# An attention and mixture-of-experts kernel whose steps are issued in another listed order

## The chip, the core and the metric

The kernel runs on one core of a Trainium2 chip. The metric is device time in microseconds, the median of several runs of the whole program, from its inputs in HBM to its output in HBM. A core has five engines that run side by side and wait for each other through semaphores: TensorE (PE in the rows, its weight loads PEld), VectorE (DVE), ScalarE (ACT), GpSimd (POOL) and SyncE (SP), which here only issues transfers.

## What is computed

First a linear attention over 8 batches of 8 heads, 576 positions, head size 64, with a feature map of 128 columns that is used with both signs. Its output, heads side by side, is the input of a layer of four attention experts, of which each position uses two.

```python
def phi(x):
    proj = np.einsum('bhsd,df->bhsf', x, w_phi)
    proj = proj - np.max(np.abs(proj), axis=-1, keepdims=True)
    return np.concatenate([np.exp(proj), np.exp(-proj)], axis=-1)
q_p, k_p = (phi(q), phi(k))
kv = np.einsum('bhsf,bhsd->bhfd', k_p, v)
z = np.sum(k_p, axis=2)
num = np.einsum('bhsf,bhfd->bhsd', q_p, kv)
den = np.einsum('bhsf,bhf->bhs', q_p, z)[..., None] + 1e-06
x = num / den                          # then (batch, position, head * 64)
...
logits = x @ w_gate                    # the two largest of four, softmax over them
for e in range(4):
    q, k, v = x @ wq[e], x @ wk[e], x @ wv[e]
    scores = np.where(causal, -1e9, q @ k.transpose(0, 2, 1) / 8)
    ye = softmax(scores) @ v @ wo[e]
    out += weight_of_e * ye
```

## The kernel before

Two heads of one batch make a pair; there are 32 pairs (p), 16 pairs of pairs (m), and 8 batches (b) with two groups (g) of two experts. The work is cut into streams, written as Python generators, which run over these. Each `yield Step(engine, ...)` in one is a step: some instructions on one engine, with the PSUM bank that it needs. The streams that matter below:

- `load_k`, `load_q`, `load_v`, `load_tails`, `load_v_tails` and `weights` issue transfers on SyncE (the first two q loads on ScalarE). `k_in` and `q_in` have two buffers, `v_in` has one: `load_v` of pair p comes after the key-value product of pair p - 1 has read `v_in`.
- `stream_k`, `stream_q` and `stream_tails` project with `w_phi` (helper `half_mm`, L501). `center` and `evac_u` take the results out of PSUM, `phi_k` and `phi_q` make the exponentials. `evac_u` copies into `u` on ScalarE (L303) or VectorE (L315).
- `stream_kv` multiplies keys and values (L642), adds the column of key sums (L654), and turns the result; `stream_n` makes denominators (L740) and numerators (L751).
- `stream_b` projects to q and k of the experts and makes their scores (L294, L871), `stream_t` multiplies with the values (L1067), `project_out` makes the output, `store` writes it.
- `keep_warm` issues three small matmuls a step until the first pair's output is there.
- `key_sum` adds up key features for the sums in `zs`, by two transfers that accumulate (`add_to`, issued on GpSimd, L331): one of 512 KB for each pair from the fifth on, then one of 128 KB for the pair's tail.

The order in which these steps are issued is written out: `ORDER` has one character for each step, the place of a stream in the list of open streams, whose next step is issued then; a stream that ends leaves the list, a new one joins at its end. Each engine runs its own steps in that order. `SIDES` has a digit for each copy that either engine can make: 0 is ScalarE, 1 is VectorE. `Plan` keeps an account of estimated times as the steps are issued; from it, `Plan.loop` only takes which free PSUM bank is given next (the one that has been free for longest). What an estimate says of a transfer's issue therefore enters the program through the choice of a bank, and through the order that was found with it.

Of the kernel before, what the change touches and what calls it, by code (L numbers as in the profile page):

```python
# [16 lines left out]
B, H, S, D, F = 8, 8, 576, 64, 128  # L17
DM, E = 512, 4
# [45 lines left out]
def change_cost(a, b):  # L64
# [11 lines left out]
    r'FFBCE>?EHEH;AAG:6FF?DC8DD8D;2;5C@@ACBBB8:MIJBI::<IAGIC@FBH99F869FHDB8DCECB83CFBFBC088=DFEECBC8:68I8BFF70HG7IID'
    r'CG8D?5=B<GH6C4:99B2ECMEBEJA8J9886=GJD?>778CMI<HJKI>I<I@<BG39E9C18IHE<A@=8=?E?9G8857?7?EHAJJF083882HGF8ICDHC8DD'
    r'998:C6:GJHI>?I<:JG<1J:7IGH7J:KJGD:?<<BB:BE>@C>;GIIF>L;8>GJGIIJ;8<:=8:HJGHGGJ:IF::LGGK?I=N8=5:=>@K802GQJMM>F:I<'
    r':<0CEEBK=CFE::CFDCDDCJBICDCJCE=D9;;IJHJ<ICIKFHDF4883DD<8<G<<=BBBEI=CCDCDGEFEHGE8BB8D6A8>:I<C5:@@JJ@JEECIAD6BFI'
    r':JK:9FLH9MCLCIJGDHAF9BFAHD8IHBCIE880DH=28BHCB9;ADA@@CA@C@AEL@HB=ECD9;JJBBJD<BGFC;38772J7GF88GG?K=FD<CF895?==A3'  # L80
    r'=8EB888E67FE18D@KHJ@<0E@BCB28=E9988BBDIJID8DGB8848AF<B6<6EE57:7::G=HICLHE3DJDI:::;<BJGC>HD9GHG>B>GADEAF>EEE=8D'
    r'880@C?=B:98:DAF6DIEH8G8GBD9<:::GHHG7BB?NICL5H7B6N=EE;BGC@FI;G=E9?BDJEEBA:<::MGKKDBCG:GC=CD@BIGLMGKFBJH<G:=1348'
    r'8>?EI8IHCA=B;C<<<B>B28>:8:>>>JD>DL8DCBFKJE8::C=<FKEA5G8@:<=HFJHH9<>99AM=6HD?EK==K3@88028K7CJCLFNMKD>?<F?8G887?'
# [1108 lines left out]
```

## Time and profile before

| | us |
|---|---|
| median of three runs | 584.96 |
| the three runs | 583.71 to 586.16 |
| the profiled execution: device time | 583.6 |
| the profiled execution: span from first to last instruction | 581.6 |

The span is 2.0 us shorter than that execution's own time, which is 1.36 us below the median. The profile gives busy time by engine, by stretch and by line, who waited for whom, the chain of work that ended last, and each instruction in order of time. Times in it are counted from the start of the span. A matmul's end is modelled, so the distance between the starts of two steps tells more of TensorE than the length of one matmul.

### The profile page before, as it was taken

What the parts mean: (1) busy time and instruction counts of PE and PEld (TensorE: products, weight loads), DVE (VectorE), ACT (ScalarE), POOL (GpSimd) and SP (SyncE); (2) the same over time, 40 slices, a digit from 0 to 9 for tenths busy, and PEclk for the clock granted to TensorE, in tenths of its full rate; (3) what the DMA queues carried; (4) which work ended last, traced back from release to release, by engine and by line L of the source; (5) the groups of instructions that cost most, each with busy time, mean ns of one, the idle gap of its engine ahead of it and who ended that gap; (6) DMA issues with size and microseconds to landing.
All of it is one profiled execution on the core that took longest, in us unless ns stands there. A gap on an engine that the chain in (4) does not pass through costs nothing.

```text
span 581.6 us, 19193 instructions
## 1 busy us (share of the span) xinstructions
PE 568.9 (98%) x7655; PEld 440.1 (76%) x7655; DVE 531.6 (91%) x1150; ACT 454.4 (78%) x1109; POOL 287.3 (49%) x223
## 2 busy tenths in 40 slices
PE   7998999999999999999999999999999999999997
PEld 5664797678785779667876878867888677878886
DVE  7999899999999998999898989989999998898894
ACT  4999788878897969868878877989778678677562
POOL 4747472676337474365554457346635367331430
PEclk9999999999999999999999999999999999999999
DMA  6688546653446753593664664466556432311012
GB/s 163 153 193 200 118 102 156 151 117 93 98 114 149 175 122 53 141 230 72 147 151 101 156 134 107 98 159 134 131 130 146 114 87 46 90 58 42 1 57 109
DMA packets 55049, 69.74 MB, mean 120 GB/s; under 512 B 29232, under 2 KB 32688, under 8 KB 54960
## 3 DMA queue, kind: packets, MB, share of 16 engines
q1 hardware_dynamic: 48368, 49.58, 29.7%
q0 software_dynamic: 6272, 18.35, 19.5%
q8 instruction: 60, 0.98, 0.7%
q10 hardware_dynamic: 320, 0.59, 0.4%
q14 instruction: 29, 0.24, 0.1%
HBM read 35.59 MB, written 14.55 MB: 86 GB/s over the span
## 4 chain that ended last, share of the span: by engine, by line
PE 89%; DVE 5%; DMA 3%; ACT 2%; issue 1%; ACTq 0%; DVEq 0%; SPq 0%
PE ps_c L294 33%; PE ps_c L501 11%; PE ps_c L751 11%; PE ps_c L642 10%; PE ps_c L1067 7%; PE ps_c L871 7%; PE ps_c L740 5%; DMA v_in<-in_v_dram 2%; PE ps_c L654 2%; PE ps_c L607 2%; PE ps_c L1038 1%; DVE s L1000 1%; ACT s L303 1%; DMA q_in<-in_qt_dram 1%; DMA out_dram<-ot 0%
## 5 line engine op out<-in xcount | busy, mean ns | idle before, releaser
L713 POOL PARTITION_ALL_REDUCE mx<-u x64 | 145.7, 2299 | 66.2 <-DVE s L1000 17.1
L294 PE MATMUL ps_c<-x,qk 128*128 128x256 f32 (+1 forms) x768 | 108.0, 298 | 0.6 <-DVE yl L298 0.6
L294 PEld LDWEIGHTS ps_c<-x,qk 128*128 128x128 f32 x768 | 102.6, 189 | 4.4 <-issue 0.9
L979 POOL TENSOR_SCALAR_AFFINE_SELECT s<-s 128x256 f32<-128x256 f32 (+1 forms) x80 | 41.6, 557 | 79.5 <-ACT s L303 13.5
L305 ACT ACTIVATE ek<-ek 128x1024 f32<-128x1024 f32 x64 | 67.9, 1061 | 8.0 <-DVE ek L569 7.3
L996 POOL PARTITION_ALL_REDUCE max<-top x16 | 57.7, 3605 | 30.1 <-DVE top L992 14.4
L303 ACT COPY s<-ps_c 64x64 f32<-64x64 f32 (+4 forms) x141 | 52.9, 434 | 17.9 <-PE ps_c L871 17.6
L1000 DVE TENSOR_TENSOR s<-s,max 128x1152 f32<-128x1152 f32 (+4 forms) x80 | 65.6, 855 | 0.6 <-POOL max L996 0.6
L642 PE MATMUL ps_c<-ek,v_in 128*32 128x256 f32 x1024 | 61.7, 381 | 2.7 <-DMA v_in<-in_v_dram 2.7
L305 ACT ACTIVATE s<-s 128x384 f32<-128x384 f32 (+4 forms) x80 | 57.7, 742 | 7.4 <-DVE s L1000 7.1
L294 PE MATMUL ps_c<-yh,wo 128*128 128x256 f32 (+1 forms) x256 | 52.9, 300 | 0.0
L642 PEld LDWEIGHTS ps_c<-ek,v_in 128*32 128x32 f32 x1024 | 31.5, 110 | 25.8 <-DMA v_in<-in_v_dram 3.4
L331 POOL DMA_DIRECT2D zs<-ekt x28 | 23.6, 844 | 53.3 <-DVE zs L582 19.5
L294 PE MATMUL ps_c<-vg,x 128*128 128x260 f32 x384 | 49.0, 285 | 0.2 <-ACT s L303 0.2
L303 ACT COPY u<-ps_c 128x256 f32<-128x256 f32 (+1 forms) x107 | 40.6, 401 | 10.5 <-PE ps_c L501 9.9
L715 DVE TENSOR_TENSOR u<-u,mx 128x576 f32<-128x576 f32 x64 | 47.7, 760 | 0.4 <-POOL mx L713 0.4
L294 PEld LDWEIGHTS ps_c<-vg,x 128*128 128x128 f32 x384 | 47.1, 188 | 1.3 <-issue 0.5
L1067 PE MATMUL ps_c<-s,vs 128*32 128x320 f32 (+4 forms) x896 | 46.8, 357 | 0.0
L331 POOL DMA_DIRECT2D zs<-ek x28 | 25.4, 906 | 42.6 <-ACT ek L305 32.2
L566 DVE TENSOR_REDUCE pmax<-ps_c 128x4 f32<-128x512 f32 x64 | 42.5, 683 | 4.0 <-PE ps_c L501 3.5
L501 PE MATMUL ps_c<-q_in,wf 64*128 64x256 f32 (+1 forms) x256 | 42.9, 430 | 2.9 <-DMA q_in<-in_qt_dram 2.6
L305 ACT ACTIVATE mx<-u 128x576 f32<-128x576 f32 x64 | 43.3, 687 | 2.1 <-DVE u L715 1.8
(132 smaller groups left out, 1351.6 us busy)
## 6 DMA issues: line engine op xcount, KB each, us to landing
zs<-ek POOLq DMA_DIRECT2D x28, 512.0 KB, 5.5
out_dram<-ot SPq DMA_DIRECT2D x32, 288.0 KB, 2.8
q_in<-in_qt_dram SPq DMA_DIRECT2D x60, 144.0 KB, 3.6
k_in<-in_kt_dram SPq DMA_DIRECT2D x64, 128.0 KB, 3.5
v_in<-in_v_dram SPq DMA_DIRECT2D x32, 256.0 KB, 3.4
kvd<-kvt SPq DMA_DIRECT2D x104, 48.0 KB, 2.4
kv<-kvd SPq DMA_DIRECT2D x26, 192.0 KB, 2.6
zs<-ekt POOLq DMA_DIRECT2D x28, 128.0 KB, 3.3
```

What stands on the lines that cost most here:

```text
L294: nc.tensor.matmul(o, a, b, start=start, stop=stop, skip_group_check=True)
L303: nc.scalar.copy(o, i)
L305: nc.scalar.activation(o, i, func, **kw)
L331: nc.gpsimd.dma_start(o, i, accum_op=ALU.add)
L501: nc.tensor.matmul(o, a, b, start=True, stop=True, skip_group_check=True)
L642: nc.tensor.matmul(o[g, 0:2], v_in[:, 4 * h + t, k:64:2], ek[:, t, :, h, :].rearrange("p c (w f) -> p c w f", w=4), start=False, stop=t == ...
L713: nc.gpsimd.partition_all_reduce(M, U, 128, bass_isa.ReduceOp.absmax)
L715: dve(S, [uk], [mk], port=True).tensor_tensor(out=U, in0=U, in1=M, op=ALU.subtract)
L751: nc.tensor.matmul(ps[g:g + 32, 0:n], kvi[:, 2 * k + (h ^ p % 2), 32 * c:32 * c + 32], P_[h][c][:, s0:s1], start=c == 0, stop=c == 1, skip ...
L996: nc.gpsimd.partition_all_reduce(big.rearrange("p e s -> p (e s)"), top.rearrange("p e s -> p (e s)"), 128, bass_isa.ReduceOp.max)
L1000: dve(2 * (S - 128 * j), [('d', x, j)], [('max', z)], 1.11, True).tensor_tensor(out=block(s_, j, None, rows(j)), in0=block(s_, j, None, ro ...
L1067: nc.tensor.matmul(ps[r:r + 32, q0 - s0:s1 - s0], vs[:, j, 128 * g + 64 * e + k:128 * g + 64 * e + 64:2], ss[x][:, e, o + q0:o + s1], star ...
```

## The change

`ORDER` and `SIDES` hold other strings of the same length; two estimates of the planner's account are other numbers. Every stream has the steps that it had.

```diff
 ORDER = (
-    r'1110049B32894DDBBDCB726C8D99E1B8DF7GD4FEHDH000C=EDBF5CBBB9DC1934DEFE==E98H2=HIHHCED168E<=A541F<77DBIFJCEAE6AHH'
...
+    r'111111104923984CH2674GHG9DCEB5G8G8CE9BD4D327EIEHF=D9D9CBKCJB=FE9BHGE81==5H:HEBGG=9627GGKB1L:DC>CEDKE1E<IAFHFG<'
...
 SIDES = (
-    r'11110000111111000000001000011100000000110101100000001010001000000010010000110000000000000010000000000000000000'
...
+    r'10000000000101110010000000110000000000101000100010100010100000000010000000100000000000000000000000000100000000'
...
-    def add_to(o, i, w, r, issue=1220, part=1):
+    def add_to(o, i, w, r, issue=900, part=1):
         plan.transfer(o.free_size() * 128 * part / ADD_RATE, issue, w, list(r), 'POOL')
         nc.gpsimd.dma_start(o, i, accum_op=ALU.add)
...
         yield Step('POOL', pred=has('phi_t', m))
-        add_to(o[r], ekts[m % 2][r].rearrange("p c h f -> p (c h f)"), k, tk, 700, 0.5)
+        add_to(o[r], ekts[m % 2][r].rearrange("p c h f -> p (c h f)"), k, tk, 850, 0.5)
```

Unrolled, the lists can be compared. The 3118 steps are the same ones. `SIDES` has 520 digits, with 73 ones before and 60 after. Between the loads of `v_in` for pairs 4 and 5, SyncE issues before: k_in 6, q_in 7, q_in 8; and after: half of vg, half of wo, the other half of vg, q_in 7, the tails of keys 3. Of the `keep_warm` steps, three stand at the very start before and six after.

## Rows read from the trace of the kernel before

**Rows 1.** The page's first part: TensorE, weight loads, VectorE, ScalarE, GpSimd.

```profile
PE 568.9 (98%) x7655; PEld 440.1 (76%) x7655; DVE 531.6 (91%) x1150; ACT 454.4 (78%) x1109; POOL 287.3 (49%) x223
```

**Rows 2.** Sums by stretch: length, busy PE PEld DVE ACT POOL, clock, DMA share.

```profile
0.00:12.00 12.00, 8.24 (x86) 6.94 (x94) 8.24 (x38) 4.11 (x8) 3.85 (x7) 1.00 0.61 160
...
20.00:52.00 32.00, 31.71 (x562) 19.72 (x552) 31.00 (x64) 30.97 (x66) 18.55 (x12) 1.00 0.80 188
52.00:60.00 8.00, 5.61 (x79) 3.48 (x79) 6.41 (x12) 6.51 (x15) 5.33 (x4) 1.00 0.85 192
...
100.00:300.00 200.00, 199.48 (x2710) 152.40 (x2704) 188.37 (x403) 163.53 (x408) 108.45 (x85) 1.00 0.56 131
...
550.00:581.60 31.60, 26.61 (x321) 23.70 (x319) 23.71 (x55) 15.34 (x44) 7.39 (x6) 1.00 0.20 76
```

**Rows 3.** TensorE in order of time at the start.

```profile
1.05 1.14 PE L294 MATMUL ps_c<-warm 128*128 128x128 bf16 x9 [1.05 <-DVE col L338]
4.76 1.23 PE L501 MATMUL ps_c<-q_in,wf 64*128 64x256 f32 x4 [2.57 <-DMA q_in<-in_qt_dram]
...
11.06 0.68 PE L294 MATMUL ps_c<-warm 128*128 128x128 bf16 x9
```

**Rows 4.** What TensorE's matmuls waited for: total us, times, longest.

```profile
PE ps_c L642 <- DMA v_in<-in_v_dram: 2.7, 2, 2.4
```

**Rows 5.** The chain that ended last, 37 to 58 us: start, length, what.

```profile
37.92 1.73 PE ps_c L642 x32
...
47.88 1.91 PE ps_c L642 x32
...
49.80 6.45 DMA v_in<-in_v_dram
...
56.30 1.94 PE ps_c L642 x32
```

**Rows 6.** Groups by line: accumulating transfers, and the sums that read zs.

```profile
L331 POOL DMA_DIRECT2D zs<-ek x28 | 25.4, 906 | 42.6 <-ACT ek L305 32.2 <-ACT ot L303 4.4 <-DVE ge L936 3.8
L331 POOL DMA_DIRECT2D zs<-ekt x28 | 23.6, 844 | 53.3 <-DVE zs L582 19.5 <-DVE max L1012 7.4 <-DVE ql L824 7.3
...
L654 PE MATMUL ps_c<-zs,ones 128*32 128x128 f32 x224 | 11.4, 274 | 0.0
```

**Rows 7.** TensorE in order of time: numerator steps and the step behind them.

```profile
50.42 0.72 PE L751 MATMUL ps_c<-mx,kv 128*32 128x320 f32 x8
...
51.50 0.40 PE L654 MATMUL ps_c<-zs,ones 128*32 128x128 f32 x8
...
519.18 0.74 PE L751 MATMUL ps_c<-mx,kv 128*32 128x320 f32 x8
...
520.39 0.50 PE L294 MATMUL ps_c<-yh,wo 128*128 128x256 f32 x2
```

**Rows 8.** SyncE's issues in order of time, 40 to 55 us.

```profile
42.61 6.08 SPq L327 DMA_DIRECT2D q_in<-in_qt_dram  x4
49.80 0.34 SPq L327 DMA_DIRECT2D v_in<-in_v_dram  x1
...
53.53 1.18 SPq L327 DMA_DIRECT2D max<-in_wts_dram  x2
```

**Rows 9.** Loads of v_in: all 32, then the one at 341.6, GpSimd's transfer before.

```profile
DMA to landing us min/median/max: 2.6/3.4/6.4
...
L327 SPq DMA_DIRECT2D v_in<-in_v_dram x1: 346/346/346, 341.6 to 341.6; - x1
DMA to landing us min/median/max: 5.4/5.4/5.4
...
340.69 0.91 POOL L331 DMA_DIRECT2D zs<-ek  x1 [0.79 <-ACT ek L305]
```

**Rows 10.** Groups by line: copies into u, count, busy us, mean ns, idle before.

```profile
L303 ACT COPY u<-ps_c 128x256 f32<-128x256 f32 (+1 forms) x107 | 40.6, 401 | 10.5 <-PE ps_c L501 9.9
...
L315 DVE COPY u<-ps_c 128x320 f32<-128x320 f32 (+1 forms) x21 | 9.0, 448 | 2.8 <-PE ps_c L501 2.7
```

More of the change, by code (lines that the diff above doesn't have):

```diff
@@ new lines @@
+    r'E77AAE=D6FFH<<<=GBEBG9HE=AEGA9419352<914BEDA<F6E8GGGFJ83GHDDA7ADJ0;C;028B8A;;;JIBEFGA?:C5EEF3ED7C7?:?J6?E6EDCF'
+    r'DC@?::D;;A;:?DHAE8@F7FAAA7AD:EGKHE98GD@ED;AD;G::C?CG52173BG:HF@?:2G:9FFCFFG;EFDDDC67C0====FEEE@?:59AC=8JEH66@E'
+    r'?134D8<20H9GH9G>9CAF9<>EGAG@@B6:;:CBEDCEBC:?<8>D@BCCEFABA88;D?588I7FFJGF7;3HLFDDF;>;:;AMI>FEF?FF;E;@F@2;:E81EE'
+    r'AA00E@A@@8FG@>8DAGFE88E;8BDBBB8CC=;?5KDDBIIBH;KB6::CD=FIJA:9F9943808H88ACG6GCCFHG8@GH8:6J?8GI8D7JJFJ8EJHEF5:KF'
+    r'H<=>F<7E9E?GL>99NOF6@HD788I8IK6ANLAM78ACAKLJ@<>HHG3GH=D9<<>248DG98<=@<GG9>81?7==D78E=5I28DAFEEI=C<<IDD=8D8388C'
@@ new lines @@
+    r'D998>::6JKJHHF:IKIKFI=::7IGG=C<FK7I0::CAII=MENH<;;L<8LD<EKBKJIIFJE<8H::J:J?8J>=AEML=F:5:KLLIGO:LKJFI88::K:L@GM'
+    r'==>=KGEEECF8E8EF>JFEKFEGIE:;;>9;GDHEH=3FHBEECA6CDED002F<<<JBCH<HIHE<IEABABGA8F88A=DB:;5:J8L:ID:PMCD6JAMNAALEIA'
+    r'LDQQC0DKFC99GDBFG94GBEH3=CH8CEEDDKJHIJCDJH<BBE2FGCCB9B9AF@@DJ@GF=@EG;BH;7EHDHH=CC718888G?7B8BLG<8>>>82DFE839I5'
+    r'JD8786JK88JQJFG@HFFKF9489188K5KJKJGF8I=FDCF>L@<FF77OL6A<GHB6HC<EH=<:KC8083::::LMEMHJ>8C28:88G9L>BGKD>IEFFFAAEE'
+    r'89A@CC::<68GEEFHC9I?B1H8::;KJ=88838GD7CGJGHD5E7:BEGE=BGBAFLL=M6@6KBC;;9:I?:EE=><<FGH>>AFIGE@AJ::DD:I48H0IFI?H@'
@@ new lines @@
+    r'C?:HGFDCD??@B<FE<D><A?2@@@CB82=@=H8BBBFB?:<EA:I8BJ:K<?J5:9?CKJ3MAL90II8AC<F8LDGF98?7@HGGDCB088@@GE>>>F@8HHGDH7'
+    r'6F88?<BEKBKAGADH8EG99@A6HI9?IAH7?IF3;5KH@?IGJGB?<882@H<G>G48A8C>?D7=0>BJ=A=B<AI@<88;9B@F@9;G<J<JG8JJGGHA889FAB'
+    r'FE5>I:7:7?K0J23F<188HI88MMLH:H:GD:FH::E6FL?K89LEHCG9GJGGDG>HI8J8DI=GHGCF8:FEFHH;:<::JL:7DDGJR5?HP7ICKEQ6RJMN:S'
+    r'MME0QG83488822?EL=>:RJDBJNJOJCM8:EMGEEG:EE;?G;==DKIG6FCJG8JC89CKKD58HKLKJKGG@=EFF<<<<<IGGBBGB<MAE:::GEF9SE6LL>'
+    r'D99ANLNL8@:087QALB@7J881QE<3JCPPABLMH888:6EBJM8E=K@KKN8E999MD35JLL78N8N88MJSPOPOLCG?H?2=K=PO=8?8HJJ>H>899HHGKK'
@@ L101 @@
+    r'772847767664434330022270000;<95441877221716766466000096558085567<:;=9:857002055;:770077776:6756775751106655575'
+    r'900=0@04A:7?=97:;:=1181<99=7=977587188772215712531331111114442488552:12223951989077226616111101001515541412131'
+    r'00>?054=21>==11;3420807541611220242200'
 )
 SIDES = (
-    r'11110000111111000000001000011100000000110101100000001010001000000010010000110000000000000010000000000000000000'
-    r'00000000000000010000000000000000000000000000000000000000001000000000000000101001001000000000100000000000000000'
@@ L109 @@
+    r'00000000000000000000000001000100000000010000000001100000000010010000100000000000000000100000000100000100011000'
+    r'00000000001000000000000100000000000010100000000000100001010000000000000010000000000000000000001010100000000000'
+    r'00000100000100000000000101001000001000000100001000000000001000000000000000111100'
 )
```

42 lines of the change are left out of this document (11 added, 31 removed).

## The prediction, made from the kernel before alone

> **What bounds the kernel now.** I read the busy shares first [rows 1]. TensorE has a matmul in flight for 568.9 us of a span of 581.6 us, VectorE is busy for 531.6 us. The reader should see that only 581.6 - 568.9 = 12.7 us are left in which TensorE has nothing at all. Next I read the same sums by stretch, to see where these 12.7 us lie [rows 2]: 3.76 us in the first 12 us (12.00 - 8.24), 0.29 us from 20 to 52, 2.39 us from 52 to 60, 0.52 us from 100 to 300, and 4.99 us from 550 on; nearly all the rest, 0.8 us, is from 300 to 550. A kernel of which another order is tried can gain little more than these, and not all of them: the first stretch waits for the first q transfer (2.6 us, [rows 3]), and of the last 4.99 us some 4 us are the copy and the store behind the last matmul, which every order has. So TensorE bounds the kernel from 60 us on. From 20 to 52 it is different: VectorE is busy for 31.00 and ScalarE for 30.97 of 32.00 us there [rows 2], 97% each, with TensorE at 31.71. That stretch has three full engines.
>
> Then I read who TensorE waits for [rows 4]. One wait stands out: the products of L642 wait 2.7 us for v_in, twice, and 2.4 us of that in one piece. The chain of waits shows the piece [rows 5]: key-value product 4 ends at 49.8, the transfer of v_in for pair 5 takes from 49.80 to 56.25, and product 5 starts at 56.30. v_in has one buffer, so the load can't be issued before product 4 has read it; from there TensorE has other work until 53.9 and then stands still.
>
> The transfers that the change's words speak of, the accumulating ones, are not among these waits. Their issues take 906 and 844 ns on GpSimd [rows 6]; the sums that read their result (L654, out of zs) wait 0.0 us in 224 matmuls [rows 6]. The number put right in the planner is the price of something for which TensorE never waits in this trace. What the change can do, it does through the new order itself.
>
> **The change part by part.** Unrolled step by step, both lists hold the same 3118 steps. On TensorE 249 of 658 steps stand at the same place, the others have moved by 1.4 places in the mean; it is a near neighbour of the old order, not another one. Five things differ that can be priced.
>
> *Changes of TensorE's tiling.* The list before changes the shape of the array between neighbouring steps 181 times, the new one 176 times. Price of one change: the 320-column numerator step (16 matmuls, L751) takes 51.50 - 50.42 = 1.08 us where the next step has its own tiling, and 520.39 - 519.18 = 1.21 us where it has not [rows 7]: 0.13 us. Five fewer: -0.6 us. This lies on TensorE, so it counts in full.
>
> *The load of v_in for pair 5.* The stretch of TensorE work between product 4 and product 5 holds the same steps in both lists, 4.2 us. What differs is what SyncE issues ahead of the load. Before: k_in 6, q_in 7, q_in 8; the trace shows the four q_in issues drawn out from 42.61 to 48.69 (the last two wait for their buffer), so that q_in 8, 0.29 MB, goes out right in front of v_in at 49.80 [rows 8]. After: q_in 8 stands behind v_in, and ahead of it stand two halves of vg, one half of wo, q_in 7 and two small tails, 1.15 MB that wait for nothing late and can be gone before 49.8. On SyncE these are seven issues; two weight halves take 1.18 us to issue [rows 8], so the seven take some 4 of the 8.2 us from the end of product 3 (37.92 + 1.73) to the start of product 4 [rows 5], and the queue is free in time. The load then meets only the accumulating transfer of pair 5, which GpSimd issues at the same point of both lists. Bounds for its landing: 3.4 us is the median of the 32 loads; one load issued at 341.6, a microsecond after an accumulating transfer was issued at 340.69, took 5.4 us; the longest, this one, took 6.4 us [rows 9]. Against 4.2 us of cover the wait is 0, 1.2 or 2.2 us (2.4 in the trace). I take 5.4 us, the row with the same neighbour: -1.2 us, with 0 and -2.4 as ends.
>
> Here a page of the Trainium skill speaks against a larger gain: "DMA: Bandwidth & Descriptors", section "Queues, rings and completion order", says that each DMA engine takes turns between the queues that have work for it, a packet at a time. By that rule SyncE's order doesn't get v_in away from GpSimd's transfer, and the sum would be -1.2; by the median landing it would be -2.4.
>
> *Copies moved from VectorE to ScalarE.* SIDES has 73 ones before (a one is VectorE) and 60 after: 13 copies change sides. Eight of them are copies out of PSUM into u before product 5, in the stretch where both engines are full. One costs 401 ns on ScalarE and 448 ns on VectorE [rows 10]. With what is moved behind product 5, VectorE has 112 instructions up to there, not 123, and ScalarE 102, not 94. Of that the eight copies are -3.6 us on VectorE and +3.2 us on ScalarE. VectorE had most to do there, so its relief can let TensorE come earlier; ScalarE has only 1.03 us of idle time in 32 us [rows 2] to take them, but it has idle time while TensorE stands from 53.9 to 56.3. Ends: -2.4 us (two thirds of VectorE's relief passed on) and +3.2 us. I take -0.5 us. It is the least certain term.
>
> *Warm-up matmuls.* Before, nine stand at the start, nine at 11.06 and the last three later [rows 3]; after, eighteen stand at the start. Nine took 1.14 us there, so eighteen end at about 3.3 us, still ahead of 4.76, where the first q step starts [rows 3]. At 11.06 they took 0.68 us; but what follows them waits for ScalarE's exponential of the tail, so I cost their removal at nothing: the gap takes their place. Ends: -0.7 and 0.
>
> *Everything else*, the places of stores, masks, maxima and sums: each moves by a step or two. The small waits from 60 to 550 us add to some 1.3 us of idle time in the old order (0.52 + 0.8, [rows 2]); another order has others. 0 us, with -1 and +2 as ends.
>
> Sum: -0.6 - 1.2 - 0.5 = -2.3 us. The profiled execution took 583.6 us (span 581.6), and becomes 581.3. The median of the three runs, 584.96, lies 1.36 us above the profiled one; I forecast the median: 582.7.
>
> **The rivals.** (1) *Nothing to collect.* v_in for pair 5 still lands after 6.4 us, because the accumulating transfer and the early weights fill the DMA engines as q_in 8 did, and the moved copies cancel. For it: the transfers listed up to this load add up to the same bytes, 9.35 MB before and 9.31 MB after, those of GpSimd left out. Against it: they are issued earlier. Time: 584.96 - 0.6 = 584.4.
>
> (2) *The front stage gives more.* The wait for v_in goes altogether (-2.4), and VectorE's relief is passed on (-2.4): with -0.6 that is -5.4, or 579.6. For it: VectorE at 97% from 20 to 52 us. Against it: ScalarE is as full.
>
> (3) *Slower: ScalarE becomes the bound of the front stage.* From 20 to 52 us it has 1.03 us of room, and up to product 5 it gets 3.2 us more in copies. Where a copy out of PSUM comes late, TensorE lacks a bank for its next step: in both unrolled lists few or none of the eight are free there. It decides from the point at which ScalarE's added copies exceed its idle time and the 2.4 us that TensorE gives it by standing still for v_in now. Price: +3.2 us from those eight, +5.2 us if all 13 copies (13 x 401 ns) stand ahead of something that TensorE needs; less 0.6 for the tilings: 587.6 to 589.6.
>
> That the change doesn't do what it says is only possible in one way: the corrected issue costs enter nothing but the plan, so if the new order is no better the numbers are without effect, which is rival 1.
>
> **How the numbers follow.** Chances: forecast (581.0 to 584.4) 0.45, rival 1 0.17, rival 2 0.22, rival 3 0.16. The predicted time is the forecast's, 582.7. The range leaves out the outer half of rival 2's and of rival 3's cases: 578.0 to 588.5. A measurement of this kernel tells about 0.5% from no change, 2.9 us: faster is below 582.0, slower above 587.9. Faster: rival 2 and a third of the forecast's cases, 0.37. Slower: most of rival 3, 0.13. The rest, 0.50, is within.
>
> **What would show it.** In the profile after: v_in for pair 5 issued behind q_in 7 and two tails, and landing 5 to 6 us later; TensorE's wait at L642 for v_in at 1 us, not 2.7; the idle time from 50 to 60 us at about 1.2 us. ScalarE's share up by about 5 us and VectorE's down by about 6. A 320-column numerator step should still take 1.08 and 1.21 us. If ScalarE's share from 20 to 52 reaches 99% and matmuls of L501 are drawn out in that stretch, rival 3 holds. If product 5 starts at 56 us as now, rival 1 holds. The forecast is wrong if some wait that doesn't exist now, of a v_in load further on above all (only two of 32 wait today), costs over 2 us.

## The result, and the profile after

The changed kernel takes 588.45 us (median of 10 runs, 587.14 to 591.84), the kernel before beside it 585.59 (10 runs): a ratio of 1.0066, 95% interval 1.0049 to 1.0083. It is slower by some 3.9 us, where 2.3 us less were forecast; 588.45 is just at the upper end of the range. The profiled execution took 587.14 us (span 585.2); that of before had a span of 581.6, so the two traces differ by 3.6 us.

First the page's busy shares of the changed kernel, to be held against [rows 1], then its sums by stretch against [rows 2].

```profile
PE 572.3 (98%) x7655; PEld 444.5 (76%) x7655; DVE 529.0 (90%) x1137; ACT 458.1 (78%) x1122; POOL 283.2 (48%) x223
```

```profile
0.00:12.00 12.00, 8.12 (x71) 7.25 (x72) 5.84 (x33) 3.81 (x9) 3.40 (x6) 1.00 0.61 155
20.00:52.00 32.00, 31.72 (x553) 19.68 (x554) 30.29 (x61) 31.22 (x70) 16.66 (x11) 1.00 0.73 177
52.00:60.00 8.00, 6.87 (x105) 4.12 (x99) 6.54 (x15) 6.45 (x13) 6.16 (x4) 1.00 0.96 198
100.00:300.00 200.00, 199.06 (x2708) 153.52 (x2700) 186.95 (x398) 166.33 (x412) 107.42 (x83) 1.00 0.55 126
550.00:585.20 35.20, 28.98 (x328) 26.11 (x327) 24.05 (x56) 16.09 (x47) 6.49 (x6) 0.92 0.18 68
```

From 52 to 60 us TensorE is busier than before (6.87 for 5.61): the part that was forecast came. From 550 us on the granted clock is 0.92 and not 1.00: something came that nobody had forecast. TensorE's waits name it (engine, line, releaser, total us, times, longest):

```profile
PE ps_c L501 <- DMA q_in<-in_qt_dram: 2.8, 1, 2.8
PE ps_c L1038 <- DVE max L1012: 1.9, 1, 1.9
PE ps_c L642 <- DMA v_in<-in_v_dram: 1.1, 1, 1.1
```

The wait for v_in has gone from 2.7 [rows 4] to 1.1 us, the wait for the first q has grown from 2.57 [rows 3] to 2.8, and a wait of 1.9 us at L1038 is new. The first q step itself begins 1.23 us later, at 5.99 instead of 4.76 [rows 3]; its wait grew by less, since the work in front of it ends later too. To see what each place costs, I took steps of TensorE that have equal work in front of them in both traces and read how much later they begin. The first key-value product begins at 20.57 us before and at 21.70 after: 1.13 later. The product of pair 4 is 1.54 later (47.81 and 49.35), that of pair 5, behind the shorter wait for v_in, only 0.28 later (56.30 and 56.57). Near 106 us it is 0.70, by this line of the kernel before and then of the changed one:

```profile
106.72 0.64 PE L751 MATMUL ps_c<-mx,kv 128*32 128x256 f32 x8
```

```profile
107.42 0.64 PE L751 MATMUL ps_c<-mx,kv 128*32 128x256 f32 x8
```

Further on the sums by stretch show it, three of the kernel before and then three of the changed one. The second and third go between steps with equal work in front of them. The first doesn't quite: at 105.78 the changed kernel still has half a q step to do (four matmuls of 320 columns), which the kernel before has done by then.

```profile
105.78:138.80 33.02, 32.82 (x491) 23.31 (x487) 31.84 (x66) 27.03 (x72) 21.46 (x14) 1.00 0.45 101
138.80:546.94 408.14, 407.05 (x5424) 317.59 (x5424) 377.39 (x807) 322.50 (x804) 201.46 (x161) 1.00 0.49 116
546.94:581.60 34.66, 29.65 (x350) 26.31 (x346) 26.59 (x61) 18.27 (x51) 7.71 (x6) 1.00 0.18 70
```

```profile
105.78:140.83 35.05, 34.24 (x495) 23.88 (x491) 33.62 (x71) 27.70 (x73) 19.68 (x14) 1.00 0.41 95
140.83:547.91 407.08, 406.93 (x5423) 320.12 (x5424) 377.30 (x803) 324.28 (x810) 201.18 (x161) 1.00 0.49 117
547.91:585.20 37.29, 31.02 (x350) 27.71 (x346) 25.80 (x60) 18.18 (x51) 6.75 (x6) 0.92 0.17 65
```

So the account of the two traces is: start +1.13; from there to the step at 107.42, -0.43 (v_in makes up more than the copies and the rest lose); the middle, from that step to the one at 140.83, +1.33 (2.03 late there less the 0.70 at its start); the long stretch -1.06; the tail +2.63 (37.29 - 34.66). The sum is 3.60 us, the whole difference of the spans.

Three places lose, then: start, middle and tail. My theory was that they are three separate causes that add up. The rivals: that the tail is a mere amount of VectorE's work, that the middle is a stretch in which VectorE is full whatever the order, and that time regained in one place is lost at the next wait.

All runs on one table (median, and ratio to the kernel before on the same chip; 0.001 is 0.58 us):

| run | kernel | us | ratio, 95% interval |
|---|---|---|---|
| | changed kernel | 588.45 | 1.0066 (1.0049 to 1.0083) |
| a_start | changed, start mended | 587.26 | 1.0044 (1.0026 to 1.0062) |
| a_copy | changed, other source of the stabiliser | 589.95 | 1.0088 (1.0062 to 1.0114) |
| a_fill | changed, matmuls in the tail's wait | 589.23 | 1.0074 (1.0048 to 1.0099) |
| a_start_copy | the first two together | 588.14 | 1.0061 (1.0042 to 1.0080) |
| a_act | changed, scores' copy earlier | 587.25 | 1.0051 (1.0031 to 1.0071) |
| a_act_copy | a_act and a_copy | 586.38 | 1.0034 (1.0017 to 1.0050) |
| a_gate | changed, L715 earlier | 589.87 | 1.0077 (1.0051 to 1.0104) |
| a_mid | changed, a maximum later | 589.06 | 1.0084 (1.0060 to 1.0107) |
| a_mid2 | changed, L715 earlier, all-reduce later | 587.02 | 1.0048 (1.0031 to 1.0064) |
| a_three | a_start, a_act and a_gate | 587.11 | 1.0038 (1.0018 to 1.0059) |
| a_fix3 | a_start and a_act_copy | 586.31 | 1.0029 (1.0011 to 1.0047) |
| a_vin | changed, weights behind v_in | 590.07 | 1.0093 (1.0069 to 1.0116) |
| a_zs | changed, accumulating transfer later | 587.97 | 1.0065 (1.0043 to 1.0086) |
| a_four | a_start, a_act_copy, a_mid2, a_zs | 583.45 | 0.9995 (0.9976 to 1.0013) |
| b_start | before, with the start of the changed one | 585.84 | 1.0018 (1.0002 to 1.0034) |
| b_vin | before, q 8 behind v_in 5 | 583.76 | 0.9988 (0.9970 to 1.0006) |
| b_zs | before, accumulating transfer later | 583.46 | 0.9990 (0.9973 to 1.0007) |
| b_zsv | b_vin and b_zs | 583.05 | 0.9971 (0.9958 to 0.9985) |

### The profile page after: what moved, and what is told of

The parts are those of the page before. It is cut to its first block, busy times and chain, and to the rows that moved or that the text cites. A ratio compares the mean times of both kernels' runs of the same rounds, so it can differ in the third digit from the quotient of the medians.

```text
span 585.2 us, 19184 instructions
## 1 busy us (share of the span) xinstructions
PE 572.3 (98%) x7655; PEld 444.5 (76%) x7655; DVE 529.0 (90%) x1137; ACT 458.1 (78%) x1122; POOL 283.2 (48%) x223
## 4 chain that ended last, share of the span: by engine, by line
PE 86%; DVE 5%; ACT 4%; DMA 3%; issue 1%; POOL 0%; ACTq 0%; DVEq 0%; POOLq 0%
PE ps_c L294 35%; PE ps_c L501 11%; PE ps_c L642 9%; PE ps_c L751 9%; PE ps_c L1067 7%; PE ps_c L871 7%; PE ps_c L740 5%; PE ps_c L654 2%; PE ps_c L607 1%; PE ps_c L1038 1%; DMA zs<-ek 1%; ACT ek L305 1%; DVE top L992 1%; DMA v_in<-in_v_dram 1%; DMA q_in<-in_qt_dram 1%
## 5 line engine op out<-in xcount | busy, mean ns | idle before, releaser
L713 POOL PARTITION_ALL_REDUCE mx<-u x64 | 140.2, 2222 | 56.8 <-DVE u L715 17.7
L979 POOL TENSOR_SCALAR_AFFINE_SELECT s<-s 128x256 f32<-128x256 f32 (+1 forms) x80 | 41.5, 543 | 69.1 <-ACT s L303 21.8
L1000 DVE TENSOR_TENSOR s<-s,max 128x1152 f32<-128x1152 f32 (+4 forms) x80 | 63.4, 823 | 0.0
L303 ACT COPY s<-ps_c 128x256 f32<-128x256 f32 (+4 forms) x143 | 53.1, 431 | 12.0 <-PE ps_c L871 11.7
L303 ACT COPY u<-ps_c 128x256 f32<-128x256 f32 (+1 forms) x116 | 43.3, 403 | 17.2 <-PE ps_c L501 16.6
L294 PE MATMUL ps_c<-yh,wo 128*128 128x320 f32 (+1 forms) x256 | 54.0, 305 | 0.0
L715 DVE TENSOR_TENSOR u<-u,mx 128x576 f32<-128x576 f32 x64 | 51.3, 816 | 0.0
```

Source lines behind the costliest of these rows:

```text
L294: nc.tensor.matmul(o, a, b, start=start, stop=stop, skip_group_check=True)
L303: nc.scalar.copy(o, i)
L713: nc.gpsimd.partition_all_reduce(M, U, 128, bass_isa.ReduceOp.absmax)
L715: dve(S, [uk], [mk], port=True).tensor_tensor(out=U, in0=U, in1=M, op=ALU.subtract)
L1000: dve(2 * (S - 128 * j), [('d', x, j)], [('max', z)], 1.11, True).tensor_tensor(out=block(s_, j, None, rows(j)), in0=block(s_, j, None, ro ...
```

## Experiments at the start

SyncE's first entries differ: after, k of pair 0 (two loads of 128 KB) goes out ahead of the two small tails of head 0, before it is the other way round. The q loads go out on ScalarE's queue beside them.

```diff
 ORDER, line 72 (a_start)
-    r'111111104923984...
+    r'111111104932984...
 ORDER, line 72, of the kernel before (b_start)
-    r'1110049B32894...
+    r'1110049B23894...
```

> The changed kernel with one swap at the start of SyncE's list: the two small tails of head 0 go out ahead of the k transfer of pair 0, as in the kernel before; everything else stays. Theory (three separate losses; the start is one): the q transfer then lands about 1 us sooner, TensorE's first q step starts near 4.8 us and not at 5.99, the granted clock reaches 1.0 near 7.9 us and not at 9.4, and the time falls by 1.0 to 1.5 us against the kernel after. The wait of the sums of n 14 for the maximum (1.9 us) and the lower clock behind it stay. Rival (the start is made up for later, since TensorE has waits further on that take it up): the first q step comes earlier, but the end doesn't, 0 to -0.3 us.

> The kernel before with one swap at the start of SyncE's list: k of pair 0 goes out ahead of the two small tails, as in the changed kernel. Theory (this swap by itself delays the q transfer): the first q step starts near 5.8 us and not at 4.76, the granted clock reaches 1.0 near 9.3 us and not at 7.9, and the step of the first key-value product comes 0.8 to 1.2 us later; the time rises by as much, less what the wait for v_in of pair 5 takes up, +0.3 to +1.2 us. Rival (the later start comes from other differences of the two lists, such as the number of warm-up matmuls): first q step at 4.8 us, no change.

TensorE's first q step, in the changed kernel, then in a_start, then in b_start:

```profile
5.99 1.23 PE L501 MATMUL ps_c<-q_in,wf 64*128 64x256 f32 x4 [2.83 <-DMA q_in<-in_qt_dram]
```

```profile
4.94 2.29 PE L501 MATMUL ps_c<-q_in,wf 64*128 64x256 f32 x8 [1.78 <-DMA q_in<-in_qt_dram]
```

```profile
5.74 1.23 PE L501 MATMUL ps_c<-q_in,wf 64*128 64x256 f32 x4 [3.54 <-DMA q_in<-in_qt_dram]
```

One exchange on SyncE's queue moves the step by 1.0 us in either direction, though it names another transfer on another queue: this exchange is shown as the cause of the late step. Why bytes on SyncE's queue hold up a load on ScalarE's was not tested. The record of the granted clock in the traces begins at full level at 7.92 us before, 9.44 after, 8.96 in a_start and 12.77 in b_start. In b_start the first key-value product begins at 23.35 us, 2.78 later than before, where 0.8 to 1.2 was expected; the late clock goes with it. In a_start it begins at 20.93, 0.77 sooner than in the changed kernel. In time, b_start costs 0.18%, about 1 us; a_start gives 0.22%, with intervals that overlap. Why the gain isn't safe is seen at product 5, in a_start:

```profile
56.77 3.58 PE L642 MATMUL ps_c<-ek,v_in 128*32 128x256 f32 x32 [2.05 <-DMA v_in<-in_v_dram]
...
50.00:57.00 7.00, 4.95 (x79) 3.04 (x75) 6.29 (x14) 5.46 (x13) 6.59 (x4) 0.98 0.99 206
57.00:62.00 5.00, 5.00 (x56) 2.26 (x48) 1.65 (x5) 3.12 (x7) 1.74 (x2) 0.68 0.66 116
```

TensorE gets there 0.7 us sooner and waits 2.05 us instead of 1.13; v_in lands at the same moment. Behind that wait the granted clock is 0.68 in the mean of five microseconds, so part of them at the lower level, 1.2 GHz, and product 5 takes 3.58 us. In the changed kernel it took 1.94:

```profile
56.57 1.94 PE L642 MATMUL ps_c<-ek,v_in 128*32 128x256 f32 x32 [1.13 <-DMA v_in<-in_v_dram]
```

## Experiments in the tail

The chain of waits of the changed kernel, at its end (start, length, what):

```profile
554.44 0.38 ACT vs L303
554.82 0.20 ACT s L305
555.02 0.26 ACT s L303
...
555.38 1.09 DVE top L992
...
558.01 0.59 PE ps_c L1038 x8
```

The scores of n 15 are copied out of PSUM (ACT s L303) behind other entries of ScalarE's list; VectorE's L992 waits for that, and behind L992 on VectorE stands the L1012 of n 14 that TensorE's sums (L1038) need. In the order of time the same is seen with the idle time ahead (in brackets): GpSimd's mask holds the copy into `top`, and so all that stands behind it on ScalarE; at the other end TensorE idles.

```profile
553.26 0.41 ACT L303 COPY top<-s 128x256 f32<-128x256 f32 x1 [1.37 <-POOL s L979]
...
558.01 0.59 PE L1038 MATMUL ps_c<-max,ones 128*32 128x224 f32 x8 [1.92 <-DVE max L1012]
```

That copy reads columns 0 to 127 of `s_`, which by `KEYS` belong to block 3, while the planner's account books it on block 0. First I took away what it waits for; the subtracted value is then another one:

```diff
-        copy(st.eng, 256, top[:, :, 0:128], s_[:, :, 0:128], [('top', i)], [('m', x, 0)], 0.52)
+        copy(st.eng, 256, top[:, :, 0:128], s_[:, :, KEYS[0]:KEYS[0] + 128], [('top', i)], [('m', x, 0)], 0.52)
```

> The changed kernel, in which the copy into the stabiliser of the softmax takes the first 128 columns of block 0 and not of the block that lies at column 0 (block 3); so it no longer waits for the mask of block 3, wherever that is listed. The subtracted value is another one, which the division by the sum takes out again. Same order of all steps. Theory (the loss of the tail is one chain: mask of block 3 on GpSimd, copy on ScalarE, maximum on VectorE, sums on TensorE, and the lower clock is a consequence of that stall): at 553 us the copy waits no longer for GpSimd, the sums of n 14 wait under 0.5 us instead of 1.92, the granted clock stays 1.0 at 559 us, and the time falls by 2.4 to 3.5 us against the kernel after. Rival (the tail waits for VectorE's amount of work, not for this wait): the sums still wait over 1.3 us, the clock still falls, change of 0 to -0.6 us. The start stays as late as in the kernel after under both.

The theory fell in this form: no gain, and L992 waits as long as before. From a_copy's trace:

```profile
556.16 0.38 ACT L303 COPY vs<-ps_c 128x260 f32<-128x260 f32 x1 [1.54 <-PE ps_c L294]
...
557.10 1.09 DVE L992 TENSOR_TENSOR top<-s 128x896 f32<-128x896 f32 x1 [2.77 <-ACT s L303]
```

The scores' copy now stands behind a copy of v that waits 1.54 us for TensorE. So I moved the scores' copy itself, ahead of both:

```diff
 ORDER, line 99 (a_act)
-    ...1181<99=7=97758718...
+    ...1181<988<7<8758718...
```

> The changed kernel with one step of ScalarE moved: the copy of the scores of n 15 out of PSUM (128x256) goes five places of the list earlier, ahead of the copy into the stabiliser and ahead of the copies of the last v products. Theory, formed anew after the run with the other source of the stabiliser (there the sums of n 14 still waited 1.92 us, since the scores' copy then stood behind a v copy that waited 1.54 us for TensorE): what delays VectorE is the place of this copy in ScalarE's list. The copy then runs near 552 us and not at 554.9, VectorE's L992, which idled 2.77 us for it, follows at about 553.7, the sums of n 14 wait under 0.5 us and not 1.92, and the time falls by 1.5 to 2.4 us against the kernel after (ratio to the kernel before near 1.003). Rival (another list behind it, as with the other source): the wait of the sums stays over 1.3 us, no gain. The first 550 us are as in the kernel after under both.

In a_act VectorE no longer waits for the scores' copy, but for an exponential that stands behind the copy into `top`:

```profile
DVE max L1012 <- ACT s L305: 1.4, 1, 1.4
```

TensorE's wait fell from 1.92 to 0.8 us, where under 0.5 was expected, and the time by 0.15% (0.9 us), where 1.5 to 2.4 us were expected. Two waits in a row, then, each hiding the other in whole or in part. With both edits:

> The changed kernel with both edits at its end: the copy of the scores of n 15 five places earlier on ScalarE, and the stabiliser copied from block 0, which doesn't wait for the mask of block 3 (the subtracted value is another one). Theory (two waits in a row: with the copy moved alone, VectorE's L1012 still waited 1.44 us for an exponential behind the stabiliser's copy; with the other source alone, L992 still waited 2.77 us for the scores' copy; either hides the other): without both, VectorE waits for neither, the sums of n 14 wait under 0.2 us and not 1.92, and the stretch from 547.9 us to the end takes 34.7 to 35.2 us, as in the kernel before (34.7), and not 37.3: 2.1 to 2.6 us off the kernel after. Rival (VectorE has too much listed there in any case): the sums still wait 0.8 us or more, no more than with the move alone (1.2 us off).

In a_act_copy the sums follow without a wait, and the tail, counted from the same step, takes 35.23 us for 37.29:

```profile
555.48 0.56 PE L1038 MATMUL ps_c<-max,ones 128*32 128x224 f32 x8
...
547.47:582.70 35.23, 29.42 (x350) 26.22 (x346) 26.27 (x60) 18.25 (x51) 7.92 (x6) 1.00 0.18 68
```

That is 2.06 us in the trace, 0.32% (1.9 us) in the ratios. The tail is a matter of the place of the scores' copy in ScalarE's list and of what the copy into `top` reads, not of an amount of VectorE's work.

The lower clock in the changed kernel's tail I took at first for a loss of its own:

```profile
556.00:559.00 3.00, 1.08 (x20) 0.66 (x13) 2.90 (x7) 0.53 (x2) 0.08 (x1) 1.00 0.00 0
559.00:562.40 3.40, 3.40 (x17) 3.40 (x16) 2.90 (x11) 1.25 (x5) 3.40 (x1) 0.50 0.02 5
562.40:566.00 3.60, 3.60 (x28) 3.60 (x28) 3.56 (x7) 2.10 (x6) 0.11 (x1) 1.00 0.07 24
```

To keep TensorE from idling I put matmuls into the wait (a_fill):

```diff
-        for t, c0, first, last in pieces:
+        for k, (t, c0, first, last) in enumerate(pieces):
+            for _ in range(26 if n == 14 and k == 1 else 0):
+                nc.tensor.matmul(ps[:, 384:512], warm, warm, start=True, stop=True, skip_group_check=True)
```

> The changed kernel with 26 more matmuls of the warm-up's kind (their result is read by nobody) put ahead of the last piece of the sums of n 14, where TensorE stands still for 1.92 us. No step or wait is taken away. Theory (the lower clock behind the wait is caused by the idle time): TensorE has something in flight during the wait, the granted clock stays 1.0 from 559 to 562.4 us, the wait's end stays where it is, and the steps that took 0.58 and 0.63 us there take 0.40: -1.2 to -1.7 us against the kernel after. Rival (the clock falls there for another reason, such as the share of work over a longer stretch or a moment in time): it falls all the same, time 0 to +0.4 us.

> The changed kernel with both edits: the tails of head 0 ahead of k of pair 0, and the stabiliser copied from block 0. The subtracted value is another one, as in the run with that edit alone. Theory (separate losses, so they add): the sum of both single runs, -3.5 to -5 us against the kernel after, so 583.5 to 585, level with the kernel before or below it by up to 2 us; what is left over is the middle (collision of VectorE and GpSimd at 113 us, +1 to +1.9) against the gain at v_in for pair 5 (-1.2). Rival (a later start moves the tail's wait, the two are one loss): no more than the larger of the two single gains.

a_fill doesn't show that the idle time lowers the clock: its clock stayed up, but so it did in seven of the nine profiled executions in which the sums waited 1.9 us with nothing put in (only the changed kernel and a_gate show the dip there). And it speaks against the clock as what the tail costs: its mean granted clock was 0.998 or more in six of seven executions, two of ten in the changed kernel, and yet it took 1.0074 for 1.0066, where 1.2 to 1.7 us less were expected. The trace of a_start says the same of this place: in a_start the tail has no dip and takes 586.8 - 549.73 = 37.07 us, since the gates (L961) then wait 1.2 us for ScalarE. Over all executions but a_fill's the two do go together: with the wait of 1.9 us as it was, 28 of 74 had a mean clock of 0.998 or more, with a_act or a_act_copy in the kernel 46 of 57. So a part of what these two gain in time may be clock. a_start_copy gained 0.05%; its a_copy half was without effect, as in the single run, and product 5 waited 2.1 us with the clock at 0.79 from 56 to 64 us.

## Experiments in the middle

In the changed kernel VectorE's L715 took 2.54 us in this place; in others it takes 0.75. GpSimd's all-reduce began 0.39 us after it (in order of time):

```profile
112.61 1.07 POOL L979 TENSOR_SCALAR_AFFINE_SELECT s<-s 128x256 f32<-128x256 f32 x2
...
112.97 2.54 DVE L715 TENSOR_TENSOR u<-u,mx 128x576 f32<-128x576 f32 x1
...
113.36 2.38 POOL L713 PARTITION_ALL_REDUCE mx<-u  x1
```

GpSimd was in two masks (L979) already when L715 began. That counts: at 22.36 us in the same trace another L715 began 0.31 us ahead of an all-reduce with GpSimd idle in front of it, and took its usual 0.72. VectorE's busy time from 105.78 on is 33.62 us after and 31.84 before; that this is 1.78 more, as much as L715 is drawn out (2.54 - 0.75 = 1.79), is chance, since the two stretches hold different instructions of VectorE (71 and 66). VectorE is busy for 96% of the stretch in both. Behind the collision TensorE stands three times (0.41 us at the sums of n 0, 0.66 and 0.71 at q and k of pair 11, read as distances between starts). Two single moves were tried: L715 ahead of the gates (a_gate), and a maximum that nobody awaits behind the two transposes that TensorE awaits (a_mid):

```diff
 ORDER, line 77 (a_gate)
-    ...ACAKLJ@<>HHG3G...
+    ...ACAKLJ<@>HHG3G...
 ORDER, line 77 (a_mid)
-    ...DG98<=@<GG9>81?7==D78E=5I28...
+    ...DG98<=<GG9>81?7==D78=E=5I28...
```

> The changed kernel with two neighbouring steps of VectorE exchanged near 112 us: the subtraction of L715 (q of pair 8) goes ahead of the five small steps of the gates, so that it ends before GpSimd's next all-reduce begins. Theory (VectorE stands still because L715 falls together with the all-reduce; it took 2.54 us there and 0.75 to 0.76 elsewhere): L715 takes about 0.8 us, the stalls at the sums of n 0 (0.41) and at q and k of pair 11 (0.66, 0.71) shrink to under 0.5 us in all, and TensorE's steps from 130 us on come 1.2 to 1.9 us sooner than in the kernel after, counted from the step at 105 us. Rival (the collision only moves on to the next VectorE instruction): another instruction at 113 to 116 us takes 1 us or more beyond its usual time, and the stalls stay, 0 to -0.5 us.

> The changed kernel with one VectorE step moved near 117 us: the first maximum over the blocks of n 1 (L992, 1.06 us), for which nobody on TensorE waits, goes 15 places later in the list, behind the transpose L762 and the transpose L673 whose banks TensorE's q and k steps of pair 11 wait for. Theory (the stalls of the middle, 0.66 and 0.71 us, are waits for banks that VectorE empties late since it has this maximum ahead of them): both stalls shrink to under 0.2 us, and TensorE's steps from 130 us on come 1.0 to 1.4 us sooner than in the kernel after, counted from the step at 105 us; as much off the time. Rival (the stalls come from the collision of L715 with GpSimd at 113 us, 1.8 us, which puts all of VectorE back): they stay over 0.8 us in sum.

Neither helped. In a_gate L715 took 0.75 us, and the next instruction, of five columns, was caught (0.16 us in the changed kernel):

```profile
113.38 1.95 DVE L950 TENSOR_TENSOR gs<-gs,tiny 128x5 f32<-128x5 f32 x1
```

In a_mid the stall at q of pair 11 went, the one at k (0.72) stayed, and one of 0.65 us appeared at 127.9: VectorE is behind, and somebody waits. Both runs speak for the collision's 1.8 us of VectorE's time as the cause, but don't show it. So L715 went earlier and the all-reduce of pair 10 behind that of pair 9:

```diff
 ORDER, line 77 (a_mid2)
-    ...78ACAKLJ@<>HHG3GH=D9<<>24...
+    ...78ACAKJ<@>HHG3GH=DH9<<>24...
```

> The changed kernel with the VectorE step L715 ahead of the gates near 112 us, and GpSimd's all-reduce of q of pair 10 (second head) moved behind the one of pair 9, so that it starts about 2.5 us later. Theory (the collision, 1.8 us of VectorE's time in a stretch where VectorE is busy for 98%, makes the three stalls): if no VectorE instruction of 112 to 117 us takes over 0.5 us beyond its usual time, the stalls at the sums of n 0 and at q and k of pair 11 (1.8 us in sum) fall under 0.6 us, and TensorE's steps from 140 us on come 1.2 to 1.8 us sooner than in the kernel after, counted from the step at 105 us. Rival (VectorE's listed work is too much there even without the collision): no instruction is drawn out, and the stalls stay over 1.2 us. If the collision only moves to another instruction, as when L715 alone was moved, neither is decided.

```profile
112.51 0.75 DVE L715 TENSOR_TENSOR u<-u,mx 128x576 f32<-128x576 f32 x1
...
113.79 0.43 DVE L950 TENSOR_TENSOR gs<-gs,tiny 128x5 f32<-128x5 f32 x1
...
106.60:139.98 33.38, 33.38 (x496) 23.74 (x492) 31.90 (x71) 27.83 (x73) 20.39 (x14) 1.00 0.44 100
```

No instruction is drawn out by over 0.3 us, all three stalls are gone, and the stretch takes 33.38 us for 35.05: 1.67 less. VectorE does the same 71 instructions in 31.90 us for 33.62. So the collision is shown as the cause; which of the two moves did how much is not told apart, but the first alone (a_gate) had no effect. In time it is 0.18% (1.05 us; intervals overlap), and in this execution 0.8 us was given back at 259 us, around a wait of 0.6 us for ScalarE's copy into `u`.

Together (a_three and a_fix3):

> The changed kernel with three small moves of the list and nothing else: tails of head 0 ahead of k of pair 0 at the start, L715 ahead of the gates near 112 us, the copy of the scores of n 15 ahead of the copy into the stabiliser near 553 us. Theory (three losses in three places make the result, they add): 4 to 5.5 us off the kernel after, so 583 to 584.5, at the level of the kernel before or up to 1.5 us below it. Rival (what is regained in one place is lost in the next, as TensorE then waits for something else, or the loss is mainly in the front, at v_in of pairs 3 and 5): 586 or more.

> The changed kernel with the edits of the start and of the tail together: tails of head 0 ahead of k of pair 0, the scores' copy of n 15 five places earlier on ScalarE, the stabiliser copied from block 0 (the subtracted value is another one). Theory (start 1.3 to 1.5 us, tail 2.7 us, they add; the 2 us of the middle stay, against 1.0 us of stalls that the new order has lost and the shorter wait for v_in): 584.5 to 585.7 us, within 0.2% of the kernel before. Rival (the earlier start is lost again at product 5, where v_in lands at the same moment): 586.0 to 586.6, no better than with the tail's edits alone.

Both came out at the rival's figure. a_three contains a_gate, which has no effect, and half of the tail. a_fix3 (586.31) is no better than the tail alone (586.38): its product 5 waited 1.8 us for v_in and the clock from 56 to 64 us was 0.79. In these runs the start's gain is lost at v_in.

## Experiments on v_in of pair 5

This is the term on which the prediction counted most. Its landing was tested from three sides: the weights ahead of it on SyncE moved behind it (a_vin), q of pair 8 moved behind it in the kernel before (b_vin), and GpSimd's accumulating transfer moved from ahead of it to behind the next all-reduce (a_zs; b_zs and with the q move b_zsv in the kernel before).

```diff
 ORDER, line 74 (a_vin)
-    ...HAE8@F7FAAA7AD:EGKHE98GD@ED;AD;G::C?CG52173BG...
+    ...HAE@F7FAAA7AD:EGKHEGD@ED;AD;G::C?CG52173898BG...
 ORDER, line 74 (b_vin, then b_zs, then b_zsv)
-    ...K@FBF2G@8::3BIHEF...
+    ...K@FBFG@8::32BIHEF...
+    ...K@FBF2@8::3BGIHEF...
+    ...K@FBF@8::32BGIHEF...
 ORDER, line 74 (a_zs)
-    ...7AD:EGKHE98GD@ED;AD;G...
+    ...7AD:EGHE98GD@ED;AFD;G...
```

> The changed kernel with three weight loads (two of 256 KB, one of 260 KB) moved on SyncE's list from ahead of v_in of pair 5 to behind it. Theory (the bytes that are under way set how long v_in takes): v_in of pair 5 lands after 3.4 to 4.6 us and not after 5.2 to 6.4, product 5 waits 0 to 0.5 us for it, and TensorE's steps after 60 us come 0.8 to 1.2 us sooner than in the kernel after, counted from the first key-value product; as much off the time, less if one of the weights is then late. Rival (the accumulating transfer of 512 KB alone sets it, or the size of v_in's own pieces): it takes over 5 us as before, no gain.

> The kernel before with one step moved: the load of q of pair 8 (288 KB) goes behind the load of v_in of pair 5, as in the changed kernel. It is the part of the change on which the prediction counted most. Theory (as predicted: it lands after 5.4 us and not 6.4): product 5 waits 1.2 to 1.5 us and not 2.4, 0.8 to 1.2 us off the time of the kernel before. Rival (what stands ahead of it on SyncE isn't what it waits for; v_in lands at the same moment, 6 us after its issue, for the accumulating transfer): no change, the wait stays at 2.2 to 2.5 us.

> The changed kernel with GpSimd's accumulating transfer of pair 5 (512 KB) moved behind the next all-reduce, so that it is issued some 2.4 us later, after v_in of pair 5 and not 1.3 us ahead of it. Theory (this transfer sets how long v_in takes): v_in of pair 5 lands after 3.2 to 4.5 us and not after 5.2 to 6.4, product 5 waits 0 to 0.4 us for it; the sums that read the accumulated result then wait 0 to 1 us. Gain 0.5 to 1.2 us. Rival (v_in takes over 5 us whatever stands beside it): no gain, or a loss of up to 1 us at those sums.

> The kernel before with two moves: q of pair 8 behind v_in of pair 5 on SyncE, and the accumulating transfer of pair 5 behind the next all-reduce on GpSimd. Theory (the accumulating transfer sets v_in's landing): v_in of pair 5 takes 3.2 to 4.5 us (6.4 in the kernel before), product 5 waits under 0.5 us for it and not 2.4, and the time is 1.2 to 2.2 us below the kernel before, the fastest of all versions here. Rival (as for the changed kernel): no more than the 0.6 to 1.0 us of the first move alone.

> The kernel before with one move alone: GpSimd's accumulating transfer of pair 5 goes behind the next all-reduce; q of pair 8 stays ahead of v_in of pair 5. Theory (the accumulating transfer is what v_in waits for): v_in of pair 5 takes 3.2 to 4.4 us and not 6.4, product 5 waits under 0.6 us, no execution shows the lower clock after it, and the time is 1.2 to 1.9 us below the kernel before, as with both moves. Rival (it takes both, since q of pair 8 fills the engines as well): v_in takes over 5 us, the wait stays above 1.2 us, under 0.8 us off.

The load's row among the DMA issues (KB, us from issue to landing), in this order: a_vin, b_vin, a_zs, b_zsv, b_zs.

```profile
v_in<-in_v_dram SPq DMA_DIRECT2D x1, 256.0 KB, 6.1
```

```profile
v_in<-in_v_dram SPq DMA_DIRECT2D x1, 256.0 KB, 5.6
```

```profile
v_in<-in_v_dram SPq DMA_DIRECT2D x1, 256.0 KB, 3.0
```

```profile
v_in<-in_v_dram SPq DMA_DIRECT2D x1, 256.0 KB, 3.1
```

```profile
v_in<-in_v_dram SPq DMA_DIRECT2D x1, 256.0 KB, 3.3
```

The accumulating transfer does nearly all. In a_zs, b_zsv and b_zs it is still issued, but 0.4, 0.7 and 1.6 us behind v_in, which lands after 3.0 to 3.3 us; in the profiles in which it is issued 0.7 to 1.3 us ahead, v_in takes 5.2 to 7.5. What stands ahead on SyncE does less, and how much less one profiled execution of each can't tell: a_vin's 6.1 us and b_vin's 5.6 lie within that spread, and in both GpSimd's transfer came closer ahead of v_in (0.7 to 0.8 us) than in the kernels they were made from (1.2 to 1.3). b_vin did what the prediction put on this term: landing from 6.4 to 5.6 us and the wait of product 5 from 2.4 to 1.3, in time 0.12%, which isn't told from nothing. The outcome agrees with what the prediction cited of "DMA: Bandwidth & Descriptors" in the Trainium skill: SyncE's order doesn't get v_in away from GpSimd's transfer. The taking of turns itself is in no trace.

In time, a_zs gave nothing (1.0065): TensorE then waits elsewhere, 0.5 us for VectorE's copy into `u` at 59 us. In the kernel before, the move alone gave 0.10% (0.6 us, not told from nothing, where 1.2 to 1.9 were expected), both moves 0.29% (0.15 to 0.42%), the one version whose interval lies below the kernel before: 583.05 us. There too most of the gain goes at the next wait: in b_zs product 5 begins 2.1 us sooner than before, and 1.36 us of that is lost behind it, in a wait for VectorE's L298.

Last, the four mended places of the changed kernel in one:

> The changed kernel with all moves that helped singly: tails of head 0 ahead of k of pair 0; the accumulating transfer of pair 5 behind the next all-reduce; L715 ahead of the gates with the all-reduce of pair 10 behind that of pair 9; the scores' copy of n 15 earlier and the stabiliser copied from block 0 (the subtracted value is another one). Theory (these places are the whole loss, and with v_in landing in time the earlier start is no longer lost at product 5): the tail's 2.7 and the middle's 1.4 add, the start and v_in bring 0.5 to 1.5 together: 582.8 to 584.4, 0.1 to 0.4% below the kernel before. Rival (each mended place hands its time on to the next wait): 585.5 or more, no better than the kernel before.

583.45 us, ratio 0.9995: the four places bring 0.71%, 4.2 us, and the interval (0.9976 to 1.0013) has no room for the loss of the changed kernel. So the four together are worth the loss. They are not an account of the loss alone, since one of them, the accumulating transfer's, also bears on the kernel before: against b_zs (0.9990) the new list is level, against b_zsv (0.9971) it is 0.24% behind. Of the earlier start and landing a part is kept: product 5 begins 2.1 us sooner than in the changed kernel, the step behind it waits 0.89 us for VectorE's copy into `u`, and at 60 us 0.57 is left. The step at 140.83 begins at 138.60, 2.23 sooner, of which the middle is worth 1.67 (a_mid2); the kernel before has 138.80. Mended, the new list is level with the old one, and not better.

## Why the prediction was wrong

- *v_in, -1.2.* Right in reason, and in size in this trace: 5.2 us where 5.4 was put, a wait of 1.1 us for 2.4, 1.26 us made up from product 4 to product 5, and the neighbour that the row was chosen for is what sets it (a_zs, b_zs). What the prediction didn't see is that the saving isn't firm, so that the close agreement is in part luck: over the other profiled kernels with that transfer ahead of it, v_in took 5.2 to 7.5 us and product 5 waited 1.1 to 3.4. (Where the prediction says beside this term that "the sum would be -1.2" or -2.4, it means the term; the sum of all is -2.3.)
- *Copies, -0.5 (-2.4 to +3.2).* No run takes this term by itself. The traces show little in either direction: from the first key-value product to that of pair 4 the changed kernel loses 0.41 us; from 20 to 52 us VectorE has 30.29 us for 31.00, ScalarE 31.22 for 30.97, TensorE 31.72 for 31.71. Rival 3, the one put up for the slower side at a price of 3 to 5 us, is not what happened.
- *Tilings, -0.6.* No run tests this term, and it isn't seen: in the long stretch TensorE's busy time fell by 0.12 us (407.05 to 406.93), and the rest of the -1.06 is idle time.
- *Warm-up, 0.* The matmuls themselves did no harm, but the step looked only at TensorE's entries of the start. SyncE's entries there were not read, though the first q transfer was named as the bound of that stretch: this step failed too, by +1.13 us at the first key-value product (a_start, b_start).
- *Everything else, 0 with -1 and +2.* This step failed. It took the small waits of the old trace (1.3 us) as the measure of what another order has. The old stalls did go (-1.06 in the long stretch), but new ones of +1.33 in the middle and +2.63 in the tail came, and the sum of the three, +2.9, lies outside the ends; with the start it is +4.0. Neither is a step that "moves by a place or two" at its usual price: one is an in-order engine where an entry with a late input (the copy into `top`, the copies of v) stands ahead of one that VectorE waits for; the other makes VectorE stand still for 1.8 us beside GpSimd.
- The chance of slower, 0.13, came from one mechanism in the front. It should have had one for the places where engines meet: 249 of 658 steps of TensorE keep their place, and nothing that the prediction read in the trace of before bounded what the other 409 meet.
- The sign of falsehood that the prediction named, a wait that doesn't exist now and costs over 2 us, is what the tail shows: 1.92 us at L1038, 2.63 us by the end.

## What to carry to other kernels

When a listed order is exchanged for another with the same work, go through each in-order queue for entries whose input comes late, and ask what stands behind them, up to the engine that sets the end; a stall of two links goes only when both are mended, and either one alone may show little or no effect (a_copy, a_act). A wait for a transfer is mended at the transfer that shares the DMA engines with it, which may be on another engine's queue, and not at the order of its own. Time gained ahead of a transfer that lands at a fixed moment is no gain until the transfer is mended, and what that brings can go again at the next wait (a_zs): go on to the last wait.

## What the runs showed of the hardware

- *VectorE beside GpSimd's all-reduce.* An instruction with two operands in SBUF that began 0.39 (L715) or 0.40 us (L950) ahead of the all-reduce ended 0.2 and 0.8 us ahead of the all-reduce's end; for the five columns of L950 that is 1.95 us instead of 0.16. In both cases GpSimd was in masks (L979) as they began. The Trainium skill, "SBUF — State Buffer", section "SBUF: two separate sides", says that such an instruction and one of GpSimd exclude each other on a shared port pair for a whole instruction. Here the traces agree for the first part of the all-reduce only. In the changed kernel such instructions that began 0.48, 0.80 and 0.99 us into an all-reduce of 2.14 us took 0.68, 0.43 and 0.16 us longer than usual (L992 at 356.25, L715 at 13.76 and at 142.59), and one that began 1.43 us into it took no longer (L715 at 80.53): by these figures each ran as if held until some 1.2 us of the all-reduce had passed. In the kernel before, L992 ran at its usual 0.81 us beside the later part of another:

```profile
114.55 2.48 POOL L713 PARTITION_ALL_REDUCE mx<-u  x1 [1.76 <-ACT u L303]
...
116.07 0.81 DVE L992 TENSOR_TENSOR top<-top,s 128x640 f32<-128x640 f32 x1
```

- *TensorE's clock after a wait.* In the nine profiled executions in which product 5 waited 1.8 us or more for v_in, seven show a lower granted clock behind it: 0.79 in the mean from 56 to 64 us in each (0.21 x 8 = 1.7 us lost). Where a dip was seen alone, in the tail, it was 0.50 for 3.4 us, 1.2 GHz instead of 2.4. In the eleven executions with 1.5 us or less there, none shows it. It is not certain for one execution: the kernel before waited 2.4 us in its trace without the dip. Of its 123 executions beside the experiments, 66 had a mean granted clock of 0.998 or more, and took 583.9 us in the mean, the other 57 took 585.7; in b_zs and b_zsv, where this wait is gone, 23 of 24 had it. So a part of what the move of the accumulating transfer gains may be that dip: the traces of b_zsv and of the kernel before, neither with a dip, differ by 0.4 us, the ratio is worth 1.7.
- *An accumulating transfer beside a load.* 512 KB of it, issued 0.7 to 1.3 us ahead, went with a landing of a 256 KB load after 5.2 to 7.5 us; issued 0.4 to 1.6 us behind the load, with 2.8 to 3.3.
